# Bucketed attention with two gated layers on one core: one softmax tile in six is copied into the split-operand type before its transpose, q is scaled where it is split, and the row sums of both halves are inverted together

## The chip, the cores and the metric

One core of a Trainium2 chip runs the whole program. The metric is the device time of one execution in microseconds (us); the kernel before takes 741.01 us, the median of 3 runs (741.01 to 741.36).

## The reference

Sixteen heads (2 batches of 8, 768 tokens, 64 features) go through attention in which a query sees only the keys of its own hash bucket; the result, 1536 tokens of 512 features, goes through two layers of width 2048. All is float32.

```python
q_bits, k_bits = (q @ proj > 0), (k @ proj > 0)        # 6 bits make a bucket
scores = where(q_bucket == k_bucket, q @ k.T / 8, -1e9)
attn = exp(scores - max); attn = attn / (sum(attn) + 1e-9)
x = (attn @ v) as 1536 x 512
h = x @ w_in;  g = h * tanh(softplus(h));  x = g @ w_out     # layer 1
h = x @ w_in2; g = h - tanh(h);            out = g @ w_out2  # layer 2
```

## The kernel before, in words

**Numbers.** TensorE multiplies in float32r, which keeps fewer bits than float32. So most operands are split: a high part (a cast to float32r) and a low part (the rest), and a product is made of two or three float32r products. float32 appears on TensorE in one place alone: the transposes of softmax tiles (L643).

**Attention.** A pair is two heads of one batch (8 pairs, index g); `h` is the head in it, `half` a half of its 768 queries. `halves_split` splits q and k; `piece` multiplies them with the hash planes and makes signs of the result; `stack` copies parts of both into the operands a, b, c, d, with transfers on the SP queue, so that one product yields masked scores. `scores` handles a tile of 128 queries by 768 keys: four matmuls (L582, L583) into the one buffer `s`, on VectorE a minimum with the row minimum kept (L586), on ScalarE the exponential with the row sum kept (L609). A half-head has three such tiles `p`. `chunk` transposes 128 keys of all three (L643, three transposes), casts the result to `ph` (ScalarE, L659) and forms the low part `pl` (VectorE, L662); three of the 12 chunks of a head go by GpSimd instead (L651, L655). `product` multiplies them with the values (L622, L623). At the end `gather` adds two halves of the result, `inverse` turns row sums into reciprocals and spreads them over partitions by way of DRAM (SP transfers `inv<-rt`, `r<-inv`), and `finish` scales and splits the result (GpSimd).

Except for pair 0, q is first scaled in place on ScalarE (L423), then cast (L430), and its low part formed on GpSimd (L454). Pair 0 does it in one pass each: a scaled cast (L434) and a fused low part on VectorE (L444).

**The layers.** About 500 us of float32r products with the same kind of splits. Nothing of this part is edited by itself.

**What sets the order.** Nothing is issued as written. Each step is recorded by `op` with an engine, an assumed cost, a priority (`key`) and what it reads and writes; `Plan.order` (L196) then simulates the engines with these costs and writes every engine's instructions in the order of the simulated starts. `dma` records transfers, of which nearly all go to SP, whose queue is served in order. Each engine does too. The table of numbers at the head of the file (assumed costs and latencies, leads such as `AHEAD`, the ticks by which the scores go ahead of the transposes, and `PV_LAG`, the chunks by which products lag) thus moves instructions on all engines, in the layers too. Tiles are numbered as they are first written in that order, over all engines: a tile with a higher number was taken later.

Of the kernel before, what the change touches and what calls it, by code (L numbers as in the profile page):

```python
# [38 lines left out]

POOL_C = ((1, 4), (4,))  # L40
POOL_LAST = ((4,), ())
SPLIT_S = (1, 3, 5)
TAIL = 3
# [4 lines left out]
G_BUFS, E_BUFS, GX_BUFS, F_BUFS = 3, 3, 2, 2  # L48
T_BUFS, P_BUFS, U_BUFS = 4, 6, 3
RAW_BUFS = 5  # L50
RAW_LAT = 4.0
Q_SCALE = "ACT"
RATE, ISSUE = 250e3, 0.55
C_STORE, C_SPREAD = 1.3, 1.2
# [4 lines left out]

EPS = 0.0  # L60
SLOW = 0.9
SLOWP = 0.4
SPARE = 1
LATE = 0.22
LATS = 0.15
LATG = 0.5
# [3 lines left out]

TICK = 1.11
T_ATT = 8.0
M0 = 7.0
AHEAD = 9
PV_LAG = 4
PIECE = 2.5
STACK = 12
VALUES = 11
LOAD = 15
FIRST = (0.0, 1.0, 2.0, 6.0)  # L80
V_REL = 15.0
Q_REL = 9.5
Z_REL = 12.5
FILL = 3
RAW = 12.0
# [19 lines left out]
TOK_T = 3.0  # L105
CONV_A = 10
CONV_S = 24
CONV_R = 15.0
# [171 lines left out]
def tile_lsh_attention_moe(  # L280
# [57 lines left out]
    for name, tags, n in (*wd, *wb):  # L338
# [5 lines left out]
        ("stack", "a b c d", 2), ("p", "p", P_BUFS), ("vt", "vt", 3), ("gx", "ph pl", GX_BUFS),  # L344
        ("u", "u", U_BUFS), ("r", "r", 2), ("rt", "rt", 2), ("small", "mn mn2 sums", 6),
    )
# [11 lines left out]
    const, xy_p = plan.pools["const"], plan.pools["xy"]  # L358
    cst = const.tile([P, P + 66], F32, name="cst")
    ident, zb, zs, pj = cst[:, 0:P], cst[:, P:P + 1], cst[:, P + 1:P + 2], cst[:, P + 2:P + 66]  # L360
# [3 lines left out]
    tiny = const.tile([P, 2, TB], F32, name="tiny")  # L364
    const.tile([P, 72], F32, name="even")
# [3 lines left out]
    hot = plan.pools["f"].tile([P, XB], F32R, tag="f", name="hot")  # L369

    def x_tok(which, kk, t0, n):
# [41 lines left out]
    def halves_split(g, nm, halves, key):  # L413

        if (g, nm) not in stacks:
            stacks[g, nm] = [buf("tqk", nm + n, [P, S], F32R) for n in ("h", "l")]
        raw, (th, tl) = raws[g, nm], stacks[g, nm]
        for i in halves:
            c = slice(i * HB, (i + 1) * HB)
            k0 = key + 0.2 * i  # L420
            if nm == "q" and g:
                if Q_SCALE == "ACT":
                    op("ACT", 0.42, k0 - 0.1, lambda c=c: nc.scalar.activation(out=raw()[:, c], in_=raw()[:, c], func=AF.Copy, scale=-SCALE), [], [(raw, i)])  # L423
                else:
                    op(
                        "POOL", 0.5, k0 - 0.1, lambda c=c: nc.gpsimd.tensor_scalar(
                            out=raw()[:, c], in0=raw()[:, c], scalar1=-SCALE, scalar2=0.0, op0=ALU.mult, op1=ALU.add
                        ), [], [(raw, i)],
                    )
                op("ACT", 0.42, k0, lambda c=c: nc.scalar.copy(th()[:, c], raw()[:, c]), [(raw, i)], [(th, i)])  # L430
            elif nm == "q":
                op(
                    "ACT", 0.38, k0, release=Q_REL if (g, i) == (0, 1) else 0.0, fn=
                    lambda c=c: nc.scalar.activation(out=th()[:, c], in_=raw()[:, c], func=AF.Copy, scale=-SCALE),  # L434
                    reads=[(raw, i)], writes=[(th, i)],
                )
            elif g == 0:
                op("ACT", 0.38, k0, lambda c=c: nc.scalar.copy(th()[:, c], raw()[:, c]), [(raw, i)], [(th, i)])
            else:
                op("POOL", 0.5, k0, lambda c=c: pool_copy(th()[:, c], raw()[:, c]), [(raw, i)], [(th, i)])  # L440
            if nm == "q" and not g:
                op(
                    "DVE", 0.47 if g == 0 else 0.6, k0 + 0.1,
                    lambda c=c: nc.vector.scalar_tensor_tensor(  # L444
                        out=tl()[:, c], in0=raw()[:, c], scalar=-SCALE, in1=th()[:, c],
                        op0=ALU.mult, op1=ALU.subtract,
                    ),
                    [(raw, i), (th, i)], [(tl, i)],
                )
# [116 lines left out]
    def scores(g, h, half, t, key):  # L566
# [5 lines left out]
        p, mn = buf("p", "p", [P, S]), buf("small", "mn", [P, 1])  # L572
        sm = sums[g, half]
        rows = (False, True) if g or h else (False, True, "bits")
# [27 lines left out]
        else:  # L602
# [7 lines left out]
                out=p(), in_=p(), func=AF.Exp, bias=mn(), scale=-1.0,  # L610
                accum_out=sm()[:, h, t:t + 1],
            ),
            [mn, (p, 0), (p, 1)], [p, (sm, h, t)],
        )
        return p

# [14 lines left out]
    def chunk(g, h, half, c, ps, o, key, done):  # L631
# [13 lines left out]
        op("PE", 0.327, key, lambda: transpose(range(TB)), ps, [(pt, 0), (pt, 1)])  # L645
        if len(queue) >= PV_LAG:
# [33 lines left out]

    def inverse(g, half, key):

        sm, rd, rt = sums[g, half], rds[half], buf("rt", "rt", [P, 32])
        tok = ("rd", half)
        r = rs[g, half] = buf("r", "r", [P, HB])
        n = 2 * TB
        d = scratch.tile([2, HB], F32, name=f"inv{g}_{half}")
        used = lambda: rd[:, :n].rearrange("p (h t) -> p h t", h=2)
        op(
            "DVE", 0.15, key,  # L690
            lambda: nc.vector.tensor_tensor(out=used(), in0=sm(), in1=tiny, op=ALU.add),
            [(sm, h, t) for h in range(2) for t in range(TB)], [tok],
        )
        op("DVE", 0.18, key + 0.1, lambda: nc.vector.reciprocal(out=used(), in_=used()), [], [tok])
        op("DVE", 0.18, key + 0.2, lambda: nc.vector.transpose(out=rt(), in_=rd), [tok], [rt])

        def store():
            flat = d.rearrange("h (t x) -> (h t) x", t=TB)
            for i in range(P // 32):
                c = slice(i * 32, (i + 1) * 32)  # L700
                nc.sync.dma_start(out=flat[:, c], in_=rt()[i * 32:i * 32 + n, :])

        def spread():
            for h in range(2):
                nc.sync.dma_start(out=r()[h * D:(h + 1) * D], in_=d[h:h + 1].to_broadcast([D, HB]))

        op("DMA", C_STORE, key + 0.3, store, [rt], [("inv", g, half)])
        op("DMA", C_SPREAD, key + 0.4, spread, [("inv", g, half)], [r])

    def finish(g, half, u, key):  # L710

        b, hp = pairs[g]
        r = rs[g, half]
        t0 = b * NT + half * TB
# [3 lines left out]
        op(  # L718
            eng, cost, key + 0.2, lambda: e.tensor_tensor(out=u(), in0=u(), in1=r(), op=ALU.mult),
            [r], [(u, 0), (u, 1)],  # L720
        )
# [8 lines left out]
    for g in range(len(pairs)):  # L730
        load(g)
        k0 = at(TICKS * (g - 1)) if g else 0.0
        if g == 0:
            clear_stack()
        else:
            for n, nm in enumerate("kq"):
                halves_split(g, nm, (0, 1), k0 + PIECE * n * TICK)
# [11 lines left out]
        us = []  # L749
        for half in range(2):  # L750
            sums[g, half] = buf("small", "sums", [P, 2, TB])
            us.append(buf("u", "u", [P, HB]))
        for h in range(2):
            for half in range(2):
                n = (2 * g + h) * 2 + half
                ps = [
                    scores(g, h, half, t, at(NT * n + 2 * t - AHEAD) + 0.3) for t in range(TB)
                ]
                o = buf("ps_t", "pt", [P, 512])
                if h == 1:  # L760
                    inverse(g, half, at(NT * n - 2))

                def done(g=g, h=h, half=half, o=o, u=us[half], key=at(NT * (n + 1)) + PV_LAG):
                    gather(h, o, u, key)
                    if h == 1:
                        finish(g, half, u, key + 0.3)

                for c in range(NT):
                    chunk(g, h, half, c, ps, o, at(NT * n + c), done if c == NT - 1 else None)
# [635 lines left out]

    nc.scalar.dma_start(out=cst, in_=cst_d)
    nc.scalar.preload_act_table_set("natural_log_exp_and_others")
# [68 lines left out]
```

## Time and profile before

| | before |
|---|---|
| device time, median of 3 | 741.01 us |
| the profiled execution's own time | 740.89 us |
| span of its instructions | 739.1 us |
| mean granted TensorE clock | 0.999 |
| busy: PE, PE weight loads, DVE, ACT, POOL | 98%, 91%, 87%, 72%, 24% |

PE is TensorE, DVE VectorE, ACT ScalarE, POOL GpSimd. Matmuls overlap in the records: one that is followed by another has a duration of some hundreds of ns, while the next starts after far less. What a matmul costs in a row of them is the distance of the starts, which the chain of waits gives directly. Attention takes the first 240 us; after that POOL has nothing to do.

### The profile page before, as it was taken

The numbers are of one execution on the slowest core, as the hardware profiler recorded it, in microseconds if no ns is written. First come the engines' busy times: TensorE is split into PE (matmuls) and PEld (weight loads), VectorE is DVE, ScalarE is ACT, GpSimd is POOL, SyncE is SP. The second block draws the span as 40 slices with busy tenths as digits, with TensorE's granted clock in tenths as the row PEclk, the third lists the DMA queues.
The fourth block names the chain that finished last, engine by engine and source line by source line (L and its number), as shares of the span: only waits on it lengthen the run. The fifth ranks groups of instructions, "written<-read, shape, count | busy, mean of one in ns | idle before, by whom it ended". The sixth has DMA issues, their size and how long they took to land.

```text
span 739.1 us, 13094 instructions
## 1 busy us (share of the span) xinstructions
PE 727.7 (98%) x4382; PEld 673.6 (91%) x4382; DVE 643.8 (87%) x1372; ACT 529.7 (72%) x1140; POOL 179.7 (24%) x224
## 2 busy tenths in 40 slices
PE   7999999999999999999999999999999999999998
PEld 4889999999999999999999999998998899999997
DVE  6988998998999999999898899789898775767893
ACT  6989999999997866767676676666565445466660
POOL 5677987988961000000000000000000000000000
PEclk9999999999999999999999999999999999999999
DMA  7775775785562655545655567999986786735621
GB/s 215 184 200 130 204 201 129 204 211 126 156 175 88 231 197 168 172 156 179 204 181 186 185 232 247 330 330 329 350 295 251 270 278 232 244 144 186 222 87 64
DMA packets 59390, 150.96 MB, mean 204 GB/s; under 512 B 7990, under 2 KB 20406, under 8 KB 59324
## 3 DMA queue, kind: packets, MB, share of 16 engines
q1 hardware_dynamic: 58892, 149.65, 63.9%
q8 instruction: 34, 0.56, 0.3%
q10 hardware_dynamic: 432, 0.49, 0.2%
q14 instruction: 32, 0.26, 0.1%
HBM read 88.18 MB, written 43.04 MB: 178 GB/s over the span
## 4 chain that ended last, share of the span: by engine, by line
PE 93%; DVE 2%; DMA 2%; ACT 2%; issue 1%; POOL 0%; ACTq 0%; SPq 0%; DVEq 0%; POOLq 0%
PE pt L1023 11%; PE pt L1025 11%; PE pt L1024 11%; PE pt L643 8%; PE pt L1101 6%; PE pt L1113 6%; PE s L1100 6%; PE pt L1100 6%; PE pt L1338 5%; PE s L582 4%; PE pt L622 4%; PE pt L623 4%; PE s L583 4%; PE s L1338 3%; PE s L1113 3%; DVE p L586 1%
## 5 line engine op out<-in xcount | busy, mean ns | idle before, releaser
L1023 PE MATMUL pt<-xh,a 128*128 128x384 f32 x288 | 96.7, 336 | 0.0
L1025 PE MATMUL pt<-xh,a 128*128 128x384 f32 x288 | 96.7, 336 | 0.0
L1024 PE MATMUL pt<-xl,a 128*128 128x384 f32 x288 | 96.6, 335 | 0.0
L586 DVE TENSOR_SCALAR_CACHE_REDUCE p<-s 128x768 f32<-128x768 f32 x93 | 88.2, 948 | 7.6 <-PE s L583 5.7
L609 ACT ACTIVATE p<-p,mn 128x768 f32<-128x768 f32 x96 | 90.7, 945 | 3.1 <-DVE p L586 2.0
L662 DVE TENSOR_TENSOR pl<-pt,ph 128x384 fp32r<-128x384 f32 x148 | 78.5, 546 | 8.6 <-ACT ph L659 7.6
L643 PE MATMUL pt<-cst,p 128*128 128x128 f32 x576 | 83.8, 272 | 1.1 <-DVE pl L662 1.1
L643 PEld LDWEIGHTS pt<-cst,p 128*128 128x128 f32 x576 | 69.5, 140 | 6.1 <-DVE pl L662 1.4
L659 ACT CAST ph<-pt 128x384 fp32r<-128x384 f32 x148 | 68.8, 484 | 5.2 <-PE pt L622 3.1
L1101 PE MATMUL pt<-gh,o 128*128 128x256 f32 x256 | 71.7, 280 | 0.0
L622 PE MATMUL pt<-ph,vt 128*128 128x384 f32 x192 | 70.4, 367 | 0.3 <-ACT f L651 0.2
L582 PE MATMUL s<-b,a 128*128 128x512 f32 (+1 forms) x186 | 68.2, 367 | 1.1 <-DVE p L586 0.7
L623 PE MATMUL pt<-pl,vt 128*128 128x384 f32 x192 | 64.9, 338 | 0.4 <-DVE pl L662 0.4
L583 PE MATMUL s<-d,c 77*128 77x512 f32 (+3 forms) x186 | 59.3, 340 | 0.6 <-ACT raw L846 0.6
L802 DVE TENSOR_TENSOR gl<-pl,gh 128x384 fp32r<-128x384 f32 x96 | 52.4, 551 | 6.5 <-ACT gh L1047 6.5
L1023 PEld LDWEIGHTS pt<-xh,a 128*128 128x128 f32 x288 | 54.1, 188 | 3.3 <-ACT pl L1042 0.2
L1024 PEld LDWEIGHTS pt<-xl,a 128*128 128x128 f32 x288 | 54.1, 188 | 1.3
L1025 PEld LDWEIGHTS pt<-xh,a 128*128 128x128 f32 x288 | 54.1, 188 | 0.1
L1047 ACT CAST gh<-pl 128x384 fp32r<-128x384 f32 x96 | 48.7, 514 | 2.1 <-DVE pl L802 1.1
L1101 PEld LDWEIGHTS pt<-gh,o 128*128 128x128 f32 x256 | 48.3, 189 | 0.0
L1061 ACT COPY ph<-pt 128x384 f32<-128x384 f32 x56 | 26.9, 481 | 28.7 <-PE pt L1025 28.6
L1100 PE MATMUL pt<-gh,o 128*128 128x512 f32 x128 | 47.2, 391 | 0.0
(301 smaller groups left out, 2080.7 us busy)
## 6 DMA issues: line engine op xcount, KB each, us to landing
w<-w SPq DMA_DIRECT2D x52, 512.0 KB
raw<-in_moe_w_in_dram SPq DMA_DIRECT2D x32, 512.0 KB
raw<-in_moe_w_out_dram SPq DMA_DIRECT2D x32, 512.0 KB
split<-a SPq DMA_DIRECT2D x24, 512.0 KB
a<-split SPq DMA_DIRECT2D x24, 512.0 KB
w<-t SPq DMA_DIRECT2D x32, 256.0 KB
o<-split SPq DMA_DIRECT2D x24, 256.0 KB
b<-kh SPq DMA_DIRECT2D x30, 192.0 KB
```

What stands on the lines that cost most here:

```text
L582: nc.tensor.matmul(o, a()[:, tok], b_()[:, kc], start=True, stop=False)
L583: nc.tensor.matmul(o, c_()[used, tok], d_()[used, kc], start=False, stop=True)
L586: nc.vector.tensor_scalar(out=out, in0=in_, scalar1=MASKED, scalar2=None, op0=ALU.min, op1=ALU.min, accum_out=low)
L609: lambda: nc.scalar.activation(out=p(), in_=p(), func=AF.Exp, bias=mn(), scale=-1.0, accum_out=sm()[:, h, t:t + 1],),
L622: nc.tensor.matmul(o()[:, :HB], vt()[:, c, :], ph()[:, :HB], start=(c == 0), stop=False)
L623: nc.tensor.matmul(o()[:, :HB], vt()[:, c, :], pl()[:, :HB], start=False, stop=(c == NT - 1))
L643: nc.tensor.transpose(pt()[:, t * P:(t + 1) * P], ps[t]()[:, c * P:(c + 1) * P], ident)
L1023: nc.tensor.matmul(o, tl()[:, 0, c], at_(0, kk), start=start and kk == 0, stop=False, skip_group_check=not start)
L1024: nc.tensor.matmul(o, tl()[:, 0, c], at_(1, kk), start=False, stop=False, skip_group_check=not start)
L1025: nc.tensor.matmul(o, tl()[:, 1, c], at_(0, kk), start=False, stop=kk == 1, skip_group_check=not start)
L1100: nc.tensor.matmul(a()[:, n, :], w()[:, y, c], flat[x][:, :SEG], start=st, stop=sp)
L1101: nc.tensor.matmul(r()[:, 0, rest], w()[:, y, c], flat[x][:, SEG:], start=st and d % 2 == 0, stop=sp, skip_group_check=True)
```

## The change

- **Moved tiles.** Of the three tiles of a half-head, tile 0 of half 0 (`MOVED`), so one in six, is copied after the exponential by a 384 KB transfer on the SP queue into a second tile, of type float32r. Its six transposes then read float32r data and a float32r identity; the other five tiles stay as they are. The copies take tiles of pool `p`, which grows from 6 to 8.
- **q.** All pairs do what pair 0 did: a scaled cast on ACT and a fused low part on DVE.
- **Row sums.** For pairs 0 to 6, both halves' reciprocals are made and spread together when the second half is near its end, and both halves are finished then. Pair 7 keeps halves apart.
- **Start.** The constants land in a buffer of the layers' weights; two columns are fetched apart by a second small transfer on the ACT queue, ahead of the q loads, and the identity is cast by POOL. `FILL`, the filler matmuls ahead of the first scores, goes from 3 to 6.
- **The table** is set anew, so the order differs on all engines.

```diff
-SPLIT_S = (1, 3, 5)
+SPLIT_S = (1, 2, 4)
-T_BUFS, P_BUFS, U_BUFS = 4, 6, 3
+T_BUFS, P_BUFS, U_BUFS = 4, 8, 3
+MOVED = ((0,), ())
+MOVE_KEY = 14.8
-AHEAD = 9
-PV_LAG = 4
+AHEAD = 11
+PV_LAG = 5
...
-            if nm == "q" and g:
-                if Q_SCALE == "ACT":
-                    op("ACT", 0.42, k0 - 0.1, lambda c=c: nc.scalar.activation(out=raw()[:, c], in_=raw()[:, c], func=AF.Copy, scale=-SCALE), [], [(raw, i)])
...
-            elif nm == "q":
+            if nm == "q":
...
-            if nm == "q" and not g:
+            if nm == "q":
...
+        if t in MOVED[half]:
+            pr = buf("p", "p", [P, S], F32R)
+            dma(P * S * 4, key + MOVE_KEY, lambda: pr().bitcast(F32), p, [p], [pr], rate=FAST)
+            return pr
         return p
...
-                nc.tensor.transpose(pt()[:, t * P:(t + 1) * P], ps[t]()[:, c * P:(c + 1) * P], ident)
+                o, x = pt()[:, t * P:(t + 1) * P], ps[t]()[:, c * P:(c + 1) * P]
+                if t in MOVED[half]:
+                    nc.tensor.transpose(o.bitcast(F32R), x, ident)
+                else:
+                    nc.tensor.transpose(o, x, ident.bitcast(F32))
...
-                if h == 1:
-                    inverse(g, half, at(NT * n - 2))
+                if h == 1 and (half or g == len(pairs) - 1):
+                    inverse(g, (half,) if g == len(pairs) - 1 else (0, 1), at(NT * n - 2))
...
-    nc.scalar.dma_start(out=cst, in_=cst_d)
+    nc.scalar.dma_start(out=land[:, 0, 0:P + 66], in_=cst_d)
+    nc.scalar.dma_start(out=cst[:, 0:2], in_=cst_d[:, P:P + 2])
```

The SP queue near the start. Before, after the stack of pair 0's second head (b, d, a, c) the load of the next q follows:

```order
L381 DMA b_305<-kh_290 64x768 x2
L381 DMA k_320<-in_k_dram 128x768
L381 DMA d_335<-kl_294 64x768
L381 DMA a_350<-qh_281 64x768
L381 DMA c_364<-qh_281 64x768
L381 DMA q_382<-in_q_dram 128x768
L381 DMA a_350<-ql_287 64x768
```

Now the copy of the first tile stands there:

```order
L384 DMA b_297<-kh_286 64x768 x2
L384 DMA k_315<-in_k_dram 128x768
L384 DMA d_327<-kl_299 64x768
L384 DMA a_343<-qh_279 64x768
L384 DMA c_355<-qh_279 64x768
L384 DMA p_371<-p_345 128x768
L384 DMA q_391<-in_q_dram 128x768
L384 DMA a_343<-ql_283 64x768
```

The copy p_371 went in between c and q; no other transfer of this piece changed places.

PE where the second head of pair 2 begins its transposes. Before, three float32 tiles a chunk:

```order
L583 MATMUL s_1602<-d_1304,c_1319 128x256
L622 MATMUL pt_1589<-ph_1546,vt_1032 128x384
L623 MATMUL pt_1589<-pl_1572,vt_1032 128x384
L622 MATMUL pt_1589<-ph_1587,vt_1032 128x384
L623 MATMUL pt_1589<-pl_1599,vt_1032 128x384
L643 MATMUL pt_1621<-cst_125,p_1484 128x128
L643 MATMUL pt_1621<-cst_125,p_1539 128x128
L643 MATMUL pt_1621<-cst_125,p_1579 128x128
```

Now the first of the three reads the copy, p_1510, which the SP queue makes of p_1457 (L642 is the float32r transpose, L644 the float32 one, L619 and L620 the products):

```order
L576 MATMUL s_1590<-d_1202,c_1220 128x256
L642 MATMUL pt_1597<-ident_125,p_1510 128x128
L644 MATMUL pt_1597<-ident_125,p_1502 128x128
L644 MATMUL pt_1597<-ident_125,p_1535 128x128
L619 MATMUL pt_1583<-ph_1546,vt_955 128x384
L620 MATMUL pt_1583<-pl_1559,vt_955 128x384
L642 MATMUL pt_1610<-ident_125,p_1510 128x128
```

The chunk keeps its three transposes and its place among scores and products; its first one now waits for a transfer. Between the copy's place (1510) and this first reader (1597) the order has 35 matmuls.

## Rows read from the trace of the kernel before

**Rows 1.** Windows by stage: window, its length, busy us (x instructions), clock, DMA share, GB/s
```profile
core 0: us, PE busy (x) PEld busy (x) DVE busy (x) ACT busy (x) POOL busy (x), PEclk, DMA share, GB/s
0.00:20.00 20.00, 15.07 (x63) 10.36 (x63) 13.68 (x36) 13.53 (x26) 12.11 (x22) 1.00 0.80 221
...
65.00:215.00 150.00, 149.85 (x989) 137.51 (x988) 138.37 (x309) 145.36 (x324) 126.95 (x155) 1.00 0.68 172
...
240.00:739.00 499.00, 495.09 (x2901) 464.35 (x2899) 427.35 (x884) 308.66 (x655) 0.00 (x0) 1.00 0.64 220
```

**Rows 2.** Waits of PE, 20 to 240 us: us in total, times, longest
```profile
PE pt L643 <- DVE pl L662: 1.1, 1, 1.1
...
PE pt L622 <- DVE p L586: 0.2, 1, 0.2
```

**Rows 3.** Chain of waits: start us, us, piece; nine transposes, then float32r products
```profile
56.64 0.98 PE pt L643 x9
...
502.48 1.39 PE s L1113 x6
...
642.78 1.43 PE s L1338 x12
```

**Rows 4.** Groups of instructions: form, count, busy us, mean ns, idle before
```profile
L643 PE MATMUL pt<-cst,p 128*128 128x128 f32 x576 | 83.8, 272 | 1.1 <-DVE pl L662 1.1
L643 PEld LDWEIGHTS pt<-cst,p 128*128 128x128 f32 x576 | 69.5, 140 | 6.1 <-DVE pl L662 1.4 <-ACT p L609 0.2 <-ACT z L461 0.2
...
L622 PEld LDWEIGHTS pt<-ph,vt 128*128 128x128 f32 x192 | 36.3, 189 | 0.9 <-ACT f L651 0.4 <-POOL pl L655 0.4
L1113 PE MATMUL s<-o,gh 128*128 128x512 f32 x64 | 19.9, 392 | 0.0
L1338 PE MATMUL s<-o,gh 128*128 128x256 f32 x42 | 7.3, 282 | 0.0
L479 PEld LDWEIGHTS pt<-kh,pjl 128*64 128x64 f32 x16 | 2.3, 143 | 0.1
```

**Rows 5.** SP queue after a stack: issue at, us to issue
```profile
111.94 0.84 SPq L381 DMA_DIRECT2D c<-z  x1
112.83 0.50 SPq L381 DMA_DIRECT2D q<-in_q_dram  x1
```

**Rows 6.** Windows over that transfer, columns as in rows 1
```profile
115.40:116.00 0.60, 0.60 (x6) 0.45 (x4) 0.60 (x1) 0.57 (x2) 0.60 (x1) 1.00 0.22 87
116.00:118.00 2.00, 1.97 (x15) 1.72 (x14) 1.92 (x6) 2.00 (x5) 1.68 (x3) 1.00 0.00 0
```

**Rows 7.** Chain of waits, first 24 us and at 41 us
```profile
0.73 0.41 ACTq L1406
1.20 3.56 DMA q<-in_q_dram
9.26 5.83 DMA d<-kl
16.69 0.66 PE pt L643 x6
41.49 5.10 DMA c<-qh
```

**Rows 8.** Groups of the q split and of the inverses, columns as in rows 4
```profile
L454 POOL TENSOR_TENSOR ql<-q,qh 128x384 fp32r<-128x384 f32 x14 | 14.1, 1016 | 1.6 <-ACT qh L430 1.6
L423 ACT ACTIVATE q<-q 128x384 f32<-128x384 f32 x14 | 7.6, 547 | 0.0
L444 DVE SCALAR_TENSOR_TENSOR ql<-q,qh 128x384 fp32r<-128x384 f32 x2 | 1.1, 556 | 1.1 <-ACT qh L434 1.1
L691 DVE TENSOR_TENSOR rd<-sums,tiny 128x6 f32<-128x6 f32 x16 | 4.0, 253 | 0.0
L695 DVE STREAM_TRANSPOSE rt<-rd 128x32 f32<-128x32 f32 x16 | 3.2, 202 | 0.0
L694 DVE RECIPROCAL rd<-rd 128x6 f32<-128x6 f32 x16 | 2.9, 180 | 0.1
```

More of the change, by code (lines that the diff above doesn't have):

```diff
@@ L369, in tile_lsh_attention_moe @@
     hot = plan.pools["f"].tile([P, XB], F32R, tag="f", name="hot")
+    land = plan.pools["w32"].tile([P, 2, DM], F32, tag="w3", name="land")
+    pj = land[:, 0, P + 2:P + 66]
     def x_tok(which, kk, t0, n):
@@ L572, in scores @@
         p, mn = buf("p", "p", [P, S]), buf("small", "mn", [P, 1])
-        sm = sums[g, half]
+        sm = sums[g]
         rows = (False, True) if g or h else (False, True, "bits")
@@ L642, in transpose @@
             for t in ts:
-                nc.tensor.transpose(pt()[:, t * P:(t + 1) * P], ps[t]()[:, c * P:(c + 1) * P], ident)
-        op("PE", 0.327, key, lambda: transpose(range(TB)), ps, [(pt, 0), (pt, 1)])
+                o, x = pt()[:, t * P:(t + 1) * P], ps[t]()[:, c * P:(c + 1) * P]
[3 more added lines that the diff above has]
+                    nc.tensor.transpose(o, x, ident.bitcast(F32))
+        op("PE", 0.327 - 0.049 * len(MOVED[half]), key, lambda: transpose(range(TB)), ps, [(pt, 0), (pt, 1)])
         if len(queue) >= PV_LAG:
@@ L679, in gather, with inverse @@
         )
[L681 to L688, printed above, removed]
+    def inverse(g, halves, key):
+        rt = buf("rt", "rt", [P, 32])
+        i0, nh = halves[0], len(halves)
+        rd, n = rds[i0], nh * 2 * TB
+        tok = ("rd", i0)
+        if (g, "r") not in rs:
+            rs[g, "r"] = buf("r", "r", [P, S])
+        r, sm = rs[g, "r"], sums[g]
+        d = scratch.tile([2, nh * HB], F32, name=f"inv{g}_{i0}")
+        used = lambda: rd[:, :n].rearrange("p (h i t) -> p h i t", h=2, i=nh)
         op(
             "DVE", 0.15, key,
-            lambda: nc.vector.tensor_tensor(out=used(), in0=sm(), in1=tiny, op=ALU.add),
-            [(sm, h, t) for h in range(2) for t in range(TB)], [tok],
+            lambda: nc.vector.tensor_tensor(out=used(), in0=sm()[:, :, i0:i0 + nh], in1=tiny[:, :, :nh], op=ALU.add),
+            [(sm, h, i, t) for h in range(2) for i in halves for t in range(TB)], [tok],
         )
@@ L704, in spread @@
             for h in range(2):
-                nc.sync.dma_start(out=r()[h * D:(h + 1) * D], in_=d[h:h + 1].to_broadcast([D, HB]))
-        op("DMA", C_STORE, key + 0.3, store, [rt], [("inv", g, half)])
-        op("DMA", C_SPREAD, key + 0.4, spread, [("inv", g, half)], [r])
+                nc.sync.dma_start(out=r()[h * D:(h + 1) * D, i0 * HB:(i0 + nh) * HB], in_=d[h:h + 1].to_broadcast([D, nh * HB]))
+        op("DMA", C_STORE, key + 0.3, store, [rt], [("inv", g, i0)])
+        op("DMA", C_SPREAD, key + 0.4, spread, [("inv", g, i0)], [(r, i) for i in halves])
     def finish(g, half, u, key):
         b, hp = pairs[g]
-        r = rs[g, half]
+        r = rs[g, "r"]
         t0 = b * NT + half * TB
@@ L718, in finish @@
         op(
-            eng, cost, key + 0.2, lambda: e.tensor_tensor(out=u(), in0=u(), in1=r(), op=ALU.mult),
-            [r], [(u, 0), (u, 1)],
+            eng, cost, key + 0.2, lambda: e.tensor_tensor(out=u(), in0=u(), in1=r()[:, half * HB:(half + 1) * HB], op=ALU.mult),
+            [(r, half)], [(u, 0), (u, 1)],
         )
@@ L734, in tile_lsh_attention_moe @@
             clear_stack()
+            op("POOL", 0.25, 6.0, lambda: pool_copy(ident, land[:, 0, 0:P]))
         else:
@@ L749, in tile_lsh_attention_moe @@
         us = []
+        sums[g] = buf("small", "sums", [P, 2, 2, TB])
         for half in range(2):
-            sums[g, half] = buf("small", "sums", [P, 2, TB])
             us.append(buf("u", "u", [P, HB]))
@@ L759, in tile_lsh_attention_moe, with done @@
                 o = buf("ps_t", "pt", [P, 512])
-                if h == 1:
-                    inverse(g, half, at(NT * n - 2))
-                def done(g=g, h=h, half=half, o=o, u=us[half], key=at(NT * (n + 1)) + PV_LAG):
+                if h == 1 and (half or g == len(pairs) - 1):
+                    inverse(g, (half,) if g == len(pairs) - 1 else (0, 1), at(NT * n - 2))
+                def done(g=g, h=h, half=half, o=o, u=us[half], us=us, key=at(NT * (n + 1)) + PV_LAG):
                     gather(h, o, u, key)
-                    if h == 1:
+                    if h == 1 and g == len(pairs) - 1:
                         finish(g, half, u, key + 0.3)
+                    elif h == 1 and half:
+                        for i in range(2):
+                            finish(g, i, us[i], key + 0.3 + i)
                 for c in range(NT):
```

56 lines of the change are left out of this document (24 added, 32 removed).

## The prediction

> **What bounds the kernel now.** I read the windows by stage first. Between 65 and 215 us, inside attention, PE is busy 149.85 of 150 us, ACT 145.36, DVE 138.37 and POOL 126.95; in the layers (240 to 739 us) PE is busy 495.1 of 499 us [rows 1]. The clock column says 1.00 throughout, the full 2.4 GHz, so no clock is to be won. A busy PE can hide stalls, so I read its waits next: from 20 to 240 us five waits are recorded, 1.1 us the longest and 0.2 us the shortest [rows 2]. So TensorE's own work sets the time nearly everywhere. ACT is almost as full in attention, and only the first 20 us have real holes: PE is busy 15.07 of them [rows 1]. What the change is worth is therefore what it takes from TensorE's stream, less what it makes TensorE wait.
>
> What a matmul costs in a stream comes from the chain of waits. Nine float32 transposes take 0.98 us, 0.109 each; six float32r matmuls of 512 columns take 1.39, 0.232 each; twelve of 256 columns 1.43, 0.119 each [rows 3, 4].
>
> **The moved tiles' transposes.** There are 576 transposes [rows 4]; one in six, 96, becomes float32r. No float32r matmul of 128 columns stands in the trace. From 512 to 256 columns the cost falls by 0.113, that is 0.0565 per 128 columns, so a straight line puts 128 columns at 0.119 - 0.0565 = 0.0625 us. That would save 0.109 - 0.0625 = 0.0465 each, 96 x 0.0465 = 4.5 us in all. The other bound: the pace stays at that of the float32 transposes, and nothing is saved. For a loss the last row is that of 256 columns: at 0.119 the matmul would cost as much as one twice as wide, and 96 x 0.010 = 1.0 us would be lost. I take 4.5, since the line rests on two rows of the same type, and both fit it with new weights for every matmul.
>
> One rule speaks against it. A float32r weight load of 128 columns lasts 189 ns in the records and one of 64 columns 143, a float32 load for a transpose 140 [rows 4]: a float32r load is the longer one, and where the matmul behind it is short it may no longer hide. The Trainium skill (TensorE: Matmul & The Clock Gate, section LDWEIGHTS (loading the stationary operand)) has a load take its columns divided by 1.2 GHz, 107 ns for 128 columns; by that the transposes would go from 109 to 107 ns and the change would save an estimated 0.2 us. No run here refutes it: the closest pace with new weights for every matmul is the 119 ns of [rows 3].
>
> **The copies.** Each adds one SP issue and 384 KB. The nearest row is a load of the same size behind a stack's transfers: issued at 112.83, while the window from 116.0 on shows no DMA traffic at all, so it had landed within 3.2 us [rows 5, 6]. Three transfers on the chain were slower: 3.56 us for a half of q at the start, 5.10 and 5.83 for 192 KB pieces among others [rows 7]. So 3.2 below; above, 5.83 and 0.9 more for the second 192 KB at the 221 GB/s of that window [rows 1], 6.7. Against this stands what PE has to do between the copy's place in the order and its first reader. For p_1510 these are 35 matmuls: four groups of three transposes (4 x 0.33), three scores (3 x 0.70), four products (4 x 0.35, two matmuls of 384 columns each, 0.175 on the same line) and a piece (0.52), 5.3 us. Worked out in the same way, the 16 copies have 2.5 (the first), 5.3, then by turns 4.0, 6.0, 4.8 and 5.3, at the end 3.4 and 4.5. At 3.2 us only the first is late. I take that value, because its row has both the size and the place in the queue: 0 us for the copies in the middle. Behind a copy on SP stand loads for the next pair and transfers into next operands, wanted a pair later.
>
> **The start.** PE reaches its first transposes at 16.69 [rows 7]. In the new order two scores more stand ahead of them (2 x 0.70), so it would reach them at about 18.1. The copy p_371 is queued behind d, a and c of the stack. d is on the chain from 9.26 for 5.83 us, to 15.09; a and c take 0.9 each at 221 GB/s and the copy 1.8, so it lands at about 18.7: 0.6 us late. Besides, q is on the first chain (1.20 for 3.56 us), and the second small constant load goes ahead of it on the ACT queue, 0.41 us by the first one's issue [rows 7]; but k's second half is now cast before the copies into b, half a microsecond sooner. The filler matmuls (3 x 0.175) fall into a time in which PE waits. I take 0.7 us lost, between 3 lost and 1.5 won (one of the holes of [rows 1] closing by another order).
>
> **What costs nothing by itself.** ACT loses 14 scalings of 547 ns, 7.7 us; POOL loses 14 low parts of 1016, 14.2 us. DVE gains 14 of 556, 7.8 us, and loses 7 inverses of 253 + 180 + 202 ns, 4.4 us: 3.3 us more over attention [rows 8]. None of them is what PE waits for [rows 2], so relief brings nothing directly. DVE had 11.6 of 150 us free [rows 1]; it has room for 3.3 in 240, if with little left. The joint inverse and the later finish of the first half are wanted only by the layers; the last pair keeps its halves apart. In the layers the order shifts a little, but 495.1 of 499 us are PE work that stays [rows 1]: 0, at most 2 either way.
>
> **The sum.** 4.5 won, 0.7 lost: 3.8 us. The profiled execution took 740.89 us, 0.1 below the median of 741.01, with a span of 739.1 and 1.8 around it, so 740.9 - 3.8 = 737.1 us.
>
> **Rivals.**
> A. *Weights set the pace of the float32r transposes.* The loads of [rows 4] grow by 46 ns for 64 columns, 0.72 per column, 92 ns for 128. If a load can't overlap the one before, a transpose costs 92 to 109 ns, and 0 to 96 x 0.017 = 1.6 us are won: 740.0 to 741.6, middle 740.8. For it: those durations. Against it: the line through 512 and 256 columns shows no floor.
> B. *The copies land late.* The point from which it decides: at 4.5 us from place to landing, the waits are 2.0 + 3 x 0.5 + 1.1 = 4.6 us and all is given back. At the 5.10 of [rows 7], the copies with 4.0, 4.8, 3.4 and 2.5 us of cover are late, 9.1 us in sum: 740.9 - 4.5 + 9.1 = 745.5, slower; at 6.7 us all sixteen, 31 us: 767. For it: the DMA share of 0.68 in attention [rows 1] and two slow rows. Against it: the load of [rows 5, 6].
> C. *DVE hands its new work on.* Its 3.3 us come back as waits of PE for clamped scores or low parts: 737.1 + 3.3 = 740.4. For it: DVE at 92% and the single buffer `s`. Against it: ACT and POOL, whose relief shortens DVE's waits, and [rows 2].
> D. *The new order also closes holes.* Instead of losing 0.7 us, the start wins 2 of the 5 that PE stands idle there [rows 1]: 740.9 - 4.5 - 2 = 734.4. For it: a new order of everything. Against it: the chain there goes through transfers [rows 7], and there is one more.
>
> **How the numbers follow.** The forecast has 0.62, its own range 734.5 to 739.3 (the start's bounds, and half a microsecond of waits for copies); A 0.13, B 0.12, C 0.08, D 0.05. A measurement of this kernel tells 0.2%, 1.5 us, from no change: below 739.5 is faster, above 742.5 slower. Faster: forecast, D and a part of C and A, 0.70. Same: most of A and C and the forecast's edge, 0.18. Slower: B, 0.12. The range runs from 733.5 to 742.5: below it lies a part of D, above it B.
>
> **What would show it.** Right: the float32r transposes follow each other, and the next transpose, at about 0.06 us; PE's busy time falls by some 4 us, and waits of PE for the copied tile appear near 18 us alone. A: starts 0.09 to 0.11 apart. B: waits of PE at the first float32r transpose of a half-head, all along attention, released by a DMA. C: more waits of PE for DVE, and DVE above 95% from 65 to 215 us. The prediction is wrong if attention (the first layer product's start) does not move forward by 3 to 5 us.

## The result, and the profile after

The changed kernel is slower: 746.21 us (median of 4, 745.34 to 746.83) against 741.18 for the kernel before on the same chip, ratio 1.0063, 95% interval 1.0045 to 1.0080. The forecast was 737.1 us, with a range up to 742.5. The profiled execution took 746.29 us with a span of 744.5. "The kernel before" and "the changed kernel" are the two of the diff; runs below go by their labels, and each ratio is to the kernel before, run beside it.

The windows by stage of the changed kernel, columns as in [rows 1]:

```profile
core 0: us, PE busy (x) PEld busy (x) DVE busy (x) ACT busy (x) POOL busy (x), PEclk, DMA share, GB/s
0.00:20.00 20.00, 13.03 (x42) 8.24 (x42) 12.18 (x31) 9.48 (x18) 9.71 (x19) 0.91 0.72 185
65.00:215.00 150.00, 149.64 (x986) 132.71 (x985) 141.87 (x305) 142.35 (x313) 117.40 (x144) 1.00 0.77 197
240.00:744.50 504.50, 499.91 (x2930) 469.76 (x2928) 431.65 (x891) 311.37 (x658) 0.00 (x0) 1.00 0.63 219
```

Two things stand out against [rows 1]. In the first 20 us PE did 42 matmuls instead of 63, and the clock column says 0.91. And in the 150 us of attention PE did 986 matmuls instead of 989, though 66 of them are now the cheap float32r transposes; the busy column (149.64 against 149.85) hides this, as a busy PE can. ACT and POOL were relieved as forecast (142.35 and 117.40), DVE loaded (141.87, 94.6%).

The same kernel's first 40 us cut finer, and PE's waits of the first 16 us (total, times, longest):

```profile
0.00:10.00 10.00, 5.63 (x14) 3.34 (x14) 2.41 (x9) 3.25 (x6) 3.71 (x11) 0.98 0.57 180
10.00:20.00 10.00, 7.41 (x30) 4.90 (x28) 9.77 (x23) 6.23 (x13) 6.00 (x9) 0.84 0.87 190
20.00:40.00 20.00, 18.71 (x115) 16.35 (x115) 17.47 (x38) 17.54 (x38) 9.02 (x12) 0.92 0.73 197
```
```profile
PE pt L471 <- ACT qh L427: 2.9, 1, 2.9
PE hot_ps L1423 <- DVE hot L1417: 1.5, 1, 1.5
PE pt L473 <- DVE kl L447: 0.2, 1, 0.2
```

The wait for `qh` is new. Its origin is on the chain of waits of the changed kernel (start us, us, piece):

```profile
0.73 0.41 ACTq L1414
...
1.17 0.46 ACTq L1415
...
1.69 6.26 DMA q<-in_q_dram
...
7.98 0.53 ACT qh L427
```

Against [rows 7] the second constant load (L1415) puts q's issue from 1.20 to 1.69, and q lands 6.26 us after it instead of 3.56: at 7.95 instead of 4.76. PE stands still from 5.6 to 8.5, and then the clock is at 1.2 GHz for part of 10 to 20 and of 20 to 40 us (0.84 and 0.92 of full speed).

The moved transposes themselves, in the timeline of PE of the changed kernel (start us, us, engine, line; the busy time of one overlaps the next, so starts count):

```profile
52.50 0.23 PE L642 MATMUL pt<-ident,p 128*128 128x128 f32 x1
52.56 0.38 PE L644 MATMUL pt<-ident,p 128*128 128x128 f32 x2
```

From the float32r transpose (L642) to the next one 0.06 us, where float32 needs 0.109 [rows 3]. Of the 96, 71 have 58 to 67 ns behind them; 23 others follow a float32 transpose, start some 0.08 us early and have 0.14 behind them, which comes to the same. And the end of attention, as first and last starts of the layers' first product (the line is L1023 before and L1031 after):

```profile
L1023 PE MATMUL pt<-xh,a x288: 331/334/440, 216.1 to 705.4; 128*128 128x384 f32 x144
```
```profile
L1031 PE MATMUL pt<-xh,a x288: 331/334/346, 238.7 to 710.6; 128*128 128x384 f32 x144
```

The kernel before had 24 products of layer 1 done before its last transpose (8 starts of L1023 up to 234.5 us and as many of its two sister lines; 24 x 0.1745 = 4.2 us of work); the changed kernel has none. So the prediction's own sign speaks against it: the first layer product starts not 3 to 5 us earlier but at 238.7 us instead of 216.1, and the last transpose at 237.5 instead of 236.6.

To see where PE's time went I counted, in each stretch, every matmul at its clean pace (0.2325 us for 512 columns, 0.1745 for 384, 0.1195 for 256, 0.109 for a float32 transpose, 0.0625 for a float32r one) and took that from the stretch's length. What is left is PE's lost time, in us, from the profiled executions:

| kernel | work | 0-24 | 24-40 | 40-65 | 65-215 | 215-240 | 240-end | last matmul ends |
|---|---|---|---|---|---|---|---|---|
| before | 718.3 | 10.9 | 0.5 | 2.0 | 3.4 | 1.1 | -0.6 | 735.5 |
| changed | 714.3 | 13.7 | 2.0 | 1.6 | 6.9 | 2.8 | 0.3 | 741.5 |
| e1_copy | 714.3 | 9.9 | 1.7 | 1.3 | 7.0 | 2.2 | 0.3 | 736.7 |
| e12_f32 | 718.8 | 10.8 | 1.4 | 1.2 | 5.1 | 2.7 | 0.4 | 740.4 |
| e15_nocopy | 718.8 | 11.5 | 1.2 | 1.2 | 4.7 | 2.2 | 0.4 | 739.8 |

The work fell by 4.0 us (4.5 for the transposes, less 0.5 for three more filler matmuls): that part came true, though PE's busy time rose from 727.7 to 730.2 us. The lost time rose by 10: 2.8 at the start, 1.5 up to 40 us, 3.5 in attention, 1.7 at its end, 0.9 in the layers, less 0.4 at 40 to 65 us. A row tells of one execution: that of e1_copy had a mean clock of 1.000 and took 741.63 us, 1.8 less than its median; those of e12_f32, e15_nocopy and the changed kernel had 0.998, 0.995 and 0.995.

Where the middle loses shows in the waits of PE's weight loads, which a busy PE hides (65 to 215 us, in total, times, longest: the kernel before, e15_nocopy and the changed kernel):

```profile
PEld s L582 <- DVE p L586: 1.7, 7, 0.3
```
```profile
PEld s L575 <- DVE p L579: 3.5, 14, 0.3
```
```profile
PEld s L575 <- DVE p L579: 5.0, 17, 0.4
```

The first load of a tile's scores waits until VectorE's minimum of the tile before has emptied the one buffer `s`: 1.7 us in the old order, 3.5 in the new one (e12_f32 has 3.5 too), 5.0 with the faster transposes in it (e1_copy too).

### The profile page after: what moved, and what is told of

Its sections match the earlier page's. It is cut to its first block, busy times and chain, and to the rows that moved or that the text cites. A ratio compares the mean times of both kernels' runs of the same rounds, so it can differ in the third digit from the quotient of the medians.

```text
span 744.5 us, 13063 instructions
## 1 busy us (share of the span) xinstructions
PE 730.2 (98%) x4385; PEld 669.9 (90%) x4385; DVE 651.2 (87%) x1365; ACT 526.8 (71%) x1126; POOL 167.5 (23%) x211
## 4 chain that ended last, share of the span: by engine, by line
PE 89%; DVE 3%; ACT 3%; DMA 2%; issue 1%; SPq 0%; POOL 0%; ACTq 0%; DVEq 0%; POOLq 0%
PE pt L1031 10%; PE pt L1033 10%; PE pt L1032 10%; PE pt L1121 6%; PE s L1108 6%; PE pt L1109 6%; PE pt L644 6%; PE pt L1108 5%; PE pt L1346 5%; PE s L575 5%; PE s L576 4%; PE pt L620 4%; PE pt L619 4%; PE s L1346 3%; PE s L1121 3%; DVE p L579 1%
## 5 line engine op out<-in xcount | busy, mean ns | idle before, releaser
L1031 PE MATMUL pt<-xh,a 128*128 128x384 f32 x288 | 96.5, 335 | 0.0
L644 PE MATMUL pt<-ident,p 128*128 128x128 f32 x480 | 79.8, 274 | 0.7 <-ACT z L454 0.5
L619 PE MATMUL pt<-ph,vt 128*128 128x384 f32 x192 | 76.0, 396 | 0.3 <-ACT f L652 0.3
L620 PE MATMUL pt<-pl,vt 128*128 128x384 f32 x192 | 65.1, 339 | 0.4 <-DVE pl L663 0.4
L644 PEld LDWEIGHTS pt<-ident,p 128*128 128x128 f32 x480 | 54.5, 141 | 4.9 <-ACT f L652 0.8
L1031 PEld LDWEIGHTS pt<-xh,a 128*128 128x128 f32 x288 | 54.1, 188 | 2.8
L575 PEld LDWEIGHTS s<-b,a 128*128 128x128 f32 x186 | 35.3, 190 | 15.2 <-DVE p L579 7.8
```

What stands on the lines that cost most here:

```text
L575: nc.tensor.matmul(o, a()[:, tok], b_()[:, kc], start=True, stop=False)
L619: nc.tensor.matmul(o()[:, :HB], vt()[:, c, :], ph()[:, :HB], start=(c == 0), stop=False)
L620: nc.tensor.matmul(o()[:, :HB], vt()[:, c, :], pl()[:, :HB], start=False, stop=(c == NT - 1))
L644: nc.tensor.transpose(o, x, ident.bitcast(F32))
L1031: nc.tensor.matmul(o, tl()[:, 0, c], at_(0, kk), start=start and kk == 0, stop=False, skip_group_check=not start)
```

## The experiments

**The start: by itself, and undone.** Theory S holds the second constant load for the loss, theory M the middle of attention.

*e1_copy*: the changed kernel without that load.
```diff
-    nc.scalar.dma_start(out=cst[:, 0:2], in_=cst_d[:, P:P + 2])
     nc.vector.tensor_copy(pjh, pj)
+    nc.vector.tensor_copy(cst[:, 0:2], land[:, 0, P:P + 2])
```


> The changed kernel without its second constant load: the two columns of constants are copied on DVE out of the first load instead of being fetched by a transfer of 128 rows of 8 bytes. Theory S (that small load, ahead of q on the ACT queue, makes q land 6.26 us after its issue instead of 3.56, and PE, starved at the start, then loses clock twice): q lands by 5 us again, PE's first scores begin near 9.5 us, and the time falls by about 4 us from 746.2 to 742. Theory M (a late start is absorbed, and the loss sits between 40 and 240 us, in scores that wait for DVE and in the order of work): q lands earlier but the time stays at 745 to 746.

743.42 us, ratio 1.0035 (1.0020 to 1.0049). q lands 3.48 us after its issue, the first scores start at 9.3 us. So the load costs 0.28% of the time, 2.1 us (within some 1.7), half of what S wanted: the rest of the loss lies elsewhere.

*e2_small* and *e3_row*: the kernel before with one more load ahead of q.
```diff
     nc.scalar.dma_start(out=cst, in_=cst_d)
+    nc.scalar.dma_start(out=even[:, 0:2], in_=cst_d[:, P:P + 2])            # e2_small
+    nc.scalar.dma_start(out=even[0:1, 0:66], in_=cst_d[0:1, P:P + 66])      # e3_row
```


> The kernel before, with one transfer added on the ACT queue ahead of the q loads: the same 128 rows of 8 bytes, into a tile that nothing reads. Theory S: q lands 2 to 3 us later, and the time rises by 3 to 4.5 us, to 744 to 745.7. Theory M: it rises by under 1 us, to at most 742.

> The kernel before, with one transfer added at the same place, of one row of 264 bytes instead of 128 rows of 8. It costs ACT the same issue (0.46 us) and puts the q loads behind the same loads of the SP queue. If the small rows delay q (theory S, by the 128 packets): q lands about 0.5 us later than before, and the time is 741.2 to 741.8. If q's later issue does it (theory S, by the order in the rings: the transfers of SP get in front): q lands 2 to 3 us later and the time is 744 to 745.7, as with the small rows. Theory M: 741 to 742.

743.38 us, 1.0034 (1.0018 to 1.0050), and 744.03 us, 1.0044 (1.0029 to 1.0058). PE waits 2.9 and 3.3 us for `qh` in them, and none in the kernel before. One row of 264 bytes costs no less than 128 of 8: what counts is that q's issue slips. The chain of waits of e3_row:

```profile
1.18 0.54 ACTq L1407
...
1.78 6.05 DMA q<-in_q_dram
```

Why half a microsecond does that stands in the timeline of the kernel before:

```profile
1.20 0.90 ACTq L408 DMA_DIRECT2D q<-in_q_dram  x2
1.64 0.43 SPq L381 DMA_DIRECT2D v<-in_v_dram  x1
```

q's first half was issued 0.44 us ahead of v's 384 KB and is issued behind it in e3_row. The Trainium skill (DMA: Bandwidth & Descriptors, section Queues, rings and completion order) has each DMA engine take turns between the queues of SP and ACT, a packet at a time; the traces fit that, as q, issued behind v on the other queue, takes 2.5 us longer, but when v itself lands they do not show.

*e21_qsecond* and *e20_qfirst* tell place from presence: in the changed kernel the small load goes behind q, in the kernel before the constants' one load does.
```diff
+    for issue in early:          # the two q loads
+        issue()
     nc.scalar.dma_start(out=cst[:, 0:2], in_=cst_d[:, P:P + 2])             # e21_qsecond
     nc.scalar.dma_start(out=cst, in_=cst_d)                                 # e20_qfirst
```


> The changed kernel with its second constant load kept, but issued behind the two q loads on the ACT queue; nothing else moves. Theory S by place (q issued before v at 1.64 us lands in 3.5 us, after it in 6.3): as the kernel with the constants copied on DVE, 742.5 to 744.5. If the 128 small packets cost by themselves: 745.5 to 746.5, as the changed kernel.

> The kernel before with the constants' load issued behind the two q loads (at 1.6 us instead of 0.7). By place: q lands half a us earlier, but the constants, 128 packets of 776 bytes now issued beside v, land 1 to 3 us later than before, and PE's first pieces, which need them, begin up to 3 us late: 741 to 744. If they land in time: 739.5 to 741.

745.04 us, 1.0049 (1.0031 to 1.0066), and 742.16 us, 1.0020 (1.0009 to 1.0032). The chains of waits of e21_qsecond and of e20_qfirst, and PE's wait in the first:

```profile
2.14 8.25 DMA cst<-cst_dram
...
10.51 0.68 DVE d L457
```
```profile
PE s L577 <- DVE d L457: 2.8, 1, 2.8
```
```profile
1.65 5.46 DMA cst<-cst_dram
...
7.14 0.20 DVE pjh L1418
```

In e21_qsecond the pieces start on time (5.2 us), but now the 1 KB itself takes 8.25 us and the scores wait 2.8 us for it; in e20_qfirst the constants take 5.46 us and the pieces start at 7.5. Whichever of these loads is issued behind v lands 5.5 to 8.3 us after its issue; q ahead of it, after 3.5. So the place decides how late a load lands, and neither place tried for the second load was harmless in the trace. The time of e21_qsecond can be told neither from that of e1_copy nor from that of the changed kernel.

**The moved tiles, in an order of work that is held.** Three runs keep e1_copy's order on PE, DVE, ACT and POOL instruction by instruction.

*e12_f32*: copies stay, their transposes are float32; *e15_nocopy*: the copies go too.
```diff
-                    nc.tensor.transpose(o.bitcast(F32R), x, ident)
+                    nc.tensor.transpose(o, x.bitcast(F32), ident.bitcast(F32))    # e12_f32
-            dma(P * S * 4, key + MOVE_KEY, lambda: pr().bitcast(F32), p, [p], [pr], rate=FAST)
+            op("DMA", P * S * 4 / FAST, key + MOVE_KEY, lambda: None, [p], [pr])    # e15_nocopy, with x from p
```


> The kernel with the constants copied on DVE, in its own order, with its 16 copies, but the moved tiles' 96 transposes run as float32. Both theories: if a float32r transpose is worth its 46.5 ns at the end of the span, 4 to 4.5 us above that kernel's 743.4, so 747.4 to 748; if waits for DVE's clamps take the gain, 0 to 2 us above.

> The kernel with the constants copied on DVE, in its own order, but the 16 copies are not issued and all 576 transposes are float32 on the tiles themselves: against the run that has copies and float32 transposes in the same order (745.3 us, ratio 1.0050) it takes the copies alone away. Theory Q (a copy stands at the head of SP's queue until its exponential ends, and what is behind it is late): 2 to 4 us less, 741.5 to 743.5. If the copies are free in this order: 745 to 747.

745.29 us, 1.0050 (1.0033 to 1.0067), and 745.35 us, 1.0056 (1.0044 to 1.0069). Without the copies nothing is gained: in the new order they cost nothing that shows. And float32r is worth 0.15% and 0.21% at the end, 1.1 and 1.6 us (each within some 1.5, so the first is not clear of nothing), not 4.5: e1_copy loses 1.9 and 2.3 us more between 65 and 215 us than these two (table), and its scores wait longer for `s`. The main finding is the last row of that table of lost time. With float32 transposes, no copies and no second constant load, the changed kernel still takes 0.56%, 4.1 us, longer than the kernel before. What remains in it is the new order, q's low part on DVE, the row sums, and the rest of the new start together; no run takes these apart. Part of the 4.1 us goes with the clock: none of the six executions of e15_nocopy had a mean clock of 1.000 and ten of 17 of the kernel before beside it had, and its profile shows 0.55 and 0.77 from 15 to 25 us. At a mean clock of 1.000, two executions of e12_f32 took 742.7 and 743.5 us, those of the kernel before 740.2 to 740.7 (medians of four sets), so 2 to 3 us remain there.

*e16_noql*: e1_copy in its order, with DVE's added work left out (the low parts of q of pairs 1 to 7 are not computed).
```diff
-                    lambda c=c: nc.vector.scalar_tensor_tensor(
+                    lambda c=c: setattr(tl, "t", th()) if g else nc.vector.scalar_tensor_tensor(
```


> The kernel with the constants copied on DVE, in its own order, with the 14 low parts of q of the pairs 1 to 7 left out on DVE (the high part stands in their place): DVE loses 8 us of work, 7.7 of its 142 in 65 to 215. Theory D (DVE's load makes the scores wait for the clamps): 2 to 3 us less than that kernel's 743.4, 740.4 to 741.5. Otherwise 743 to 744.

742.89 us, 1.0024 (1.0006 to 1.0041). DVE falls from 142.05 to 135.95 us in 65 to 215 us, below the 138.37 of [rows 1], and the time by 0.8 us (within some 1.7), which is not clear of nothing. The scores' loads still wait for DVE in its trace, 6.2 us, one of them 2.0, against 5.0 in e1_copy. So the middle shows no sign that it loses by DVE's load.

**The moved tiles in the order of before.** In that order the exponential of a half's first tile ends 3.5 us (first pair) or 4.4 to 6.4 us before its first transpose, so a copy of 3.2 us has room.

*e13_hold*, *e14_hold2*: the old order on all engines, copies behind the exponentials on SP's queue, one tile in six and one in three moved. These two kernels and the next two also have e1_copy's start and its layout of the row sums.
```diff
+            if t in COPIED[half]:                      # ((0,), ()) or ((0,), (0,))
+                prs[p] = plan.pools["pr"].tile([P, S], F32R, tag="pr", name="pr")
+                nc.sync.dma_start(out=prs[p].bitcast(F32), in_=p())
...
+                    nc.tensor.transpose(o.bitcast(F32R), prs[ps[t]][:, c * P:(c + 1) * P], ident)
```


> The order of the kernel before, instruction by instruction on PE, ACT, POOL and DVE, with the copies put on SP's queue behind the exponentials of the first tile of each pair's first halves, into two buffers of their own; in that order the exponential of such a tile ends 3.4 us (first pair) or 4.5 to 6.3 us before its first transpose, and a copy lands in about 3.2. Theory O: 735.5 to 737.5, faster than before by the whole 4.5 us. If the freed PE time is handed to waits for DVE (rival C of the prediction): 739 to 741. If copies land late: 741 or more.

> As the last, with the first tile of every half moved (one in three; 192 transposes, 32 copies). Theory O: 9 us less than before if PE alone bounds the stage, 731 to 733; more likely 732 to 735, since DVE, busy 92% of 65 to 215 us before, comes close to it. If the gain is handed to waits for DVE: 738 to 741.

749.27 us, 1.0092 (1.0067 to 1.0118), and 755.55 us, 1.0170 (1.0139 to 1.0200): clearly slower, and more so with twice the tiles. Theory O, that the old order would give the whole gain, fell.

*e17_copyonly*: e13_hold, but nothing reads the copies; *e18_copyfree*: the copies come from a tile that is ready from the start.
```diff
-                    nc.tensor.transpose(o.bitcast(F32R), prs[ps[t]][:, c * P:(c + 1) * P], ident)
+                    nc.tensor.transpose(o, x, ident.bitcast(F32))
-                nc.sync.dma_start(out=prs[p].bitcast(F32), in_=p())
+                nc.sync.dma_start(out=prs[p].bitcast(F32), in_=still)               # e18_copyfree
```


> The order of the kernel before with the 16 copies in SP's queue behind their exponentials, as in the run of 749.3 us, but nothing reads the copies: all transposes are float32. Theory Q: the copies alone cost 6 us or more, 747 to 753. If it was the moved transposes that were late for their copies, or their faster pace that ran into DVE: 741 to 743.

> As the last, with 16 copies of as many bytes at the same places of SP's queue, from a tile that is ready from the start, so that they wait for no exponential. Theory Q by the wait: 741 to 743, near before. Theory Q by the bytes and the rings: 747 to 753, as with the wait.

747.97 us, 1.0092 (1.0078 to 1.0107), and 747.12 us, 1.0072 (1.0057 to 1.0087). With sixteen copies that nobody needs this order takes 6.8 us more, and 5.3 us where they wait for no exponential; that float32r gains anything here can't be told (e13_hold and e17_copyonly both have 1.0092). No run has the start and the row sums alone in this order, so that the copies do it is read from POOL's waits from 40 to 215 us, in the kernel before, in e17_copyonly and in e15_nocopy:

```profile
POOL kl L454 <- DMA d<-kl: 1.5, 3, 0.7
```
```profile
POOL kl L451 <- DMA d<-kl: 9.7, 6, 1.9
```
```profile
POOL kl L447 <- DMA d<-kl: 0.3, 1, 0.3
```

A split of k must wait until the transfer into the last pair's operand has read its buffer. The copies stand ahead of that transfer on SP's queue, and POOL waits 9.7 us instead of 1.5; POOL is late, and PE waits for its pieces (1.1 us for `kl` between 65 and 215 us, none there in the kernel before). In the new order the wait is gone (0.3 us without copies, none listed with them). So the order of before seems to have no room for 6 MB of copies, and the new order has it. Whether the making of that room is what the new order costs, no run shows.

**Orders written anew.** In these runs the planner wrote the order again, so each tells of a part and of an order.

*e4_nomove*: e1_copy with `MOVED = ((), ())`. *e5_table*: e1_copy with the old numbers but for lead, lag and buffers. *e6_before_table*: the kernel before with the new numbers (`TICK = 1.09`, `AHEAD = 11`, `PV_LAG = 5`, `STACK = 13`, `VALUES = 15`, `EPS = 0.135` and the rest of the diff's table). *e7_qsplit*: e1_copy with q's split as before. *e8_inv*: e1_copy with the row sums half by half. *e9_moved*: the kernel before with the moved tiles, and with them e1_copy's start and layout of the row sums.

> The kernel of the first run of this set (the constants copied on DVE) with no tile moved: all 768 transposes are float32, and the 32 copies by transfer are gone. If the moved transposes give their 4.5 us to the end of the span and the copies cost nothing: 4 to 5 us above the first run (746 to 747 where that one is 742). If the gain is handed on to other waits, because PE waits for DVE's clamps in the middle: 0 to 2 us above the first run.

(There are 576 transposes and 16 copies, not 768 and 32.)

> The kernel with the constants copied on DVE (743.4 us, ratio 1.0035), its order written with the numbers of the kernel before (tick, costs, keys of stacks, values and pieces, spread of the evictions); only the lead of the scores (11 ticks), the lag of the products (5) and the eight p buffers stay, which the moved tiles need. Theory T (the new numbers lose some 6 us of PE's time between 24 and 240 us): about 738, ratio 0.995 to 0.998. Theory D (DVE's added work in the split of q) and theory I (both halves' row sums inverted together, so that nothing of layer 1 can fill the end of attention): 742 to 744.

> The kernel before with the order written by the numbers of the changed kernel (lead 11, lag 5, tick, costs and keys) and no other edit; six p buffers as before. Theory T: 745 to 748 (741 and some 5 to 7 us). Theories D and I: 740.5 to 742, with at most the 0.5 us of three more filler products.

> The kernel with the constants copied on DVE, but q of the pairs 1 to 7 is scaled and copied on ACT and its low part taken on POOL, as before the change; DVE loses 14 instructions of 0.45 to 0.55 us. Theory D: 740 to 741.5 (2 to 3 us off, the waits for DVE's clamps shrink). Theory T: 743 to 744, PE's waits stay.

> The kernel with the constants copied on DVE, but the row sums are added, inverted, stored and spread for each half by itself, and the first half is finished when it is done, as before the change. Theory I: 741 to 742.4 (1 to 2.5 us off, at 215 to 240 us, with layer-1 products before the last transposes). Theories T and D: 743 to 744.5.

> Of the change, only the moved tiles (one in six, copied by a transfer and transposed as float32r; eight p buffers), on the kernel before with its numbers, its split of q and its inverses; the planner, which counts 0.049 us less per chunk and a copy more, writes the order anew (PE has 3397 of 4384 instructions in the old sequence). Theory O (each new writing of the order loses more than the 4.5 us that the transposes give): 743 to 750. Theory P (the new numbers or the parts beside the moved tiles lose it): 736 to 738.

| run | us | ratio, 95% interval |
|---|---|---|
| e4_nomove | 748.44 | 1.0100 (1.0084 to 1.0115) |
| e5_table | 752.70 | 1.0147 (1.0126 to 1.0169) |
| e6_before_table | 750.16 | 1.0125 (1.0106 to 1.0145) |
| e7_qsplit | 745.84 | 1.0060 (1.0046 to 1.0074) |
| e8_inv | 751.32 | 1.0134 (1.0116 to 1.0153) |
| e9_moved | 754.61 | 1.0168 (1.0143 to 1.0194) |

None of the gains that theories T, D and I expected came: with any single part taken back, e1_copy gets slower by 0.25 to 1.1%, and the new numbers cost the kernel before 1.25%. Parts and numbers seem to belong to each other; with an order written for another set of parts the end came 2 to 12 us later. As each of these runs has an order of its own, none shows what its part is worth. For the same reason e4_nomove's 5.0 us above e1_copy was no measure of the transposes; with the order held it is 1.1 to 1.6.

## Why the prediction was wrong

**What bounds the kernel.** Right: PE's stream sets the time in all these runs. But that PE loses nothing else, and that its clock stays, was taken as given, and the change altered just that (0.84 and 0.92 of full speed in two stretches of the first 40 us). [rows 2] lists PE's own waits; the 1.7 us that the scores' weight loads already waited for the minimum in the kernel before stand under PEld.

**The transposes' price.** Right: 0.06 us, and 4.0 us less work with the filler in. The straight line through 512 and 256 columns held, and rival A is out. The rule that spoke against it, 107 ns for a weight load (the Trainium skill, TensorE: Matmul & The Clock Gate, section LDWEIGHTS (loading the stationary operand)), does not set the pace here; the measurement decides.

**The sum, "4.5 won".** Wrong as a step: work taken out of the stream came off the end only by 1.1 to 1.6 us (e12_f32, e15_nocopy). Some 2 us of the rest turned into PE's lost time between 65 and 215 us (table), where the scores' loads wait 5.0 instead of 3.5 us for the minimum; PE's work between the scores of two tiles got shorter, the minimum between them did not (0.95 us each).

**The copies.** Right for the order that they were put in: no wait of PE for one in the middle, though a copy had 3.4 us from its issue to its first reader at the least, and no cost that shows (e15_nocopy against e12_f32). Rival B had the wrong place: in the old order PE waits 0.8 us for a copy in e13_hold, but e17_copyonly, where nothing reads them, is no faster, and there the transfers queued with them are late.

**The start, "I take 0.7 us lost".** The first failed step, and mis-sized: the second constant load was priced at its 0.41 us of issue. It costs 2.1 us in the changed kernel (within some 1.7) and 2.5 to 3.3 in the kernel before, since with it q is issued behind v and lands 3.2 us later. The trace of before had a row that hints at it, v's issue 0.44 us behind q's. The rest of the step held: in e1_copy the first transposes start at 18.6 us and wait 0.3 us for the copy, where 18.7 was forecast; in the changed kernel they start at 22.8.

**"What costs nothing by itself."** Taking DVE's added work out gave 0.8 us, within some 1.7 (e16_noql). Rival C's sign came in part: the waits for the minimum rose from 1.7 to 5.0 us, DVE only to 94.6%; but 1.8 of the 3.3 came with the order and 1.5 with the faster transposes, and without DVE's added work they stayed. No gain from the relief of ACT and POOL shows, as forecast.

**What the prediction lacked** is a price for the new order, and this is its largest failed step: the order was read for what stood ahead of the copies and the first transposes, and the rest was put at 0 ("the order shifts a little"). It costs some 4 us with q's split, the sums and the rest of the start in it (e15_nocopy, 0.44 to 0.69%): in the profiles 1.3 between 65 and 215 us, 1.0 where no layer product fills the end of attention any more, 1.3 up to 40 us, where the clock also fell, 1.0 in the layers, 0.5 for the fillers, less 0.8 at 40 to 65. Rival D expected the new order to close holes; it opened some. The ratios split the measured 4.7 us into 4.1 for the order with its parts (e15_nocopy), -1.5 for the moved tiles (from there to e1_copy) and 2.1 for the constants (from there to the changed kernel), within some 0.9, 1.4 and 1.7. The forecast had 3.8 us won, so it missed by 8.5: 4.1 for the order, 3.0 of the transposes' 4.5, and 1.4 at the start (2.1 instead of 0.7). Which number of the table opens which hole stays open: none can be changed without another order.

No version here beats the kernel before; the nearest, e20_qfirst and e16_noql (which leaves work out), are 0.2% above it.

## What to carry to other kernels

An order that a planner writes is itself a part of the change: before pricing the parts, count in the new order what fills the old one's waits, and hold the order fixed when a part is measured. Where PE is full, cheaper instructions gain only what the engines feeding it can follow. And at the start of a kernel, read the issue times of all queues side by side: a load costs not its issue but the transfer it falls behind.

## What the runs showed of the hardware that was not expected

The place of a DMA against a large one of another queue, a matter of half a microsecond at issue, decided between 3.5 and 6 us to landing; 1 KB in rows of 8 bytes took 8.25 us behind three larger loads (e21_qsecond).

Where the granted clock fell to 1.2 GHz in a profile, it did so in the first 25 us, where PE still had holes; in e13_hold and e18_copyfree instead from 200 to 215 us, where PE had stood still for 4.2 and 4.1 us. It falls in some executions of a kernel and not in others. Of e1_copy, three of 11 had a mean clock of 1.000 and took 740.9 to 741.8 us; the eight with 0.995 to 0.998 took 742.7 to 746.4. So some of the spread in every median above goes with this.

One DVE instruction, an integer operation on 128x512 words that takes 0.40 to 0.74 us in the kernel before, took 5.1 us in the profiled executions of e13_hold and e18_copyfree, both the slowest of their sets (755.7 against a median of 749.3, 754.0 against 747.1). The timeline of e13_hold:

```profile
198.09 2.00 POOL L451 TENSOR_TENSOR ql<-q,qh 128x384 fp32r<-128x384 f32 x2
...
199.56 5.10 DVE L845 TENSOR_SCALAR w<-raw 128x512 uint32<-128x512 uint32 x1
...
200.04 0.52 POOL L379 TENSOR_SCALAR ph<-f 128x384 fp32r<-128x384 f32 x1
...
201.95 1.00 POOL L733 TENSOR_TENSOR u<-u,r 128x384 f32<-128x384 f32 x1
...
203.86 0.52 POOL L379 TENSOR_SCALAR xh<-u 128x384 fp32r<-128x384 f32 x1
...
204.58 0.94 DVE L583 TENSOR_SCALAR_CACHE_REDUCE p<-s 128x768 f32<-128x768 f32 x1
```

It is issued while POOL is at work and ends just after POOL's unbroken row does, at 204.4; e18_copyfree shows the same. The Trainium skill (SBUF — State Buffer, section Who interferes with whom) says that DVE in a two-port mode and GpSimd hold their shared port for a whole instruction and the other is blocked; the trace fits that and goes further, as DVE waited for the rest of one POOL instruction and for six more. That this operation runs in such a mode no run shows, and what decides when this happens was not tried.
